# A new order, engine and bank table for a four-layer attention kernel on one core

## The chip, the core and the metric

The kernel runs on one core of a Trainium2 chip. The core has a matrix engine (TensorE, PE), a vector engine (VectorE, DVE), a scalar engine for activations (ScalarE, ACT), a general engine (GpSimd, POOL) and a sync engine (SyncE, SP), which issues most of the transfers. The engines run their own instruction streams in order and wait for each other through semaphores. Matmul results land in PSUM, which has eight banks of 128 partitions by 512 float32; everything else lives in SBUF. The metric is device time of the whole program in microseconds (us). The kernel before took 431.77 us (median of three, 431.07 to 432.0).

## The reference

x is 2048 tokens by 512 features, in bfloat16. Four residual layers follow each other, A, B, A, B, where both A layers share their weights and so do both B layers.

```python
x = x + _A_ref(_layernorm(x), A_wqkv, A_wo)
x = x + _B_ref(_layernorm(x), B_wqkv, B_wo)
x = x + _A_ref(_layernorm(x), A_wqkv, A_wo)
x = x + _B_ref(_layernorm(x), B_wqkv, B_wo)
```

Both have 32 heads of 16 features. Layer A is linear attention: phi(t) = where(t > 0, t + 1, exp(t)) + 1e-6 is applied to q and k; kv = sum over all tokens of phi(k) v; z = sum of phi(k); the output is phi(q) kv / (phi(q) z + 1e-6), times wo. Layer B is softmax attention with a causal window: a query sees its own key and the 255 before it, scores are scaled by 1/4.

## The kernel before

The 2048 tokens are 16 tiles of 128. The program is first written down as a graph of 2532 operations by the class Plan, in five parts:

- `layer_a_keys(1)`: for every tile, layernorm (`norm`: statistics on DVE, reciprocal root as `eps` and `pow` on POOL, `xn` on DVE, a transpose `T` by DMA on SP or by PE), keys and phi(k) (`a_k`, `phi`: `E` is the exp on ACT, `E1` and `phi` are on DVE), and the sums over tokens (`g`, `z`, then `gv`). Queries `a_q` go with it.
- `barrier(1)`: masks kv (`kvm`), multiplies it by wo (`M`), and forms the denominators (`den`, `rec`, `spread`, `pqd`).
- `middle(2)`: for each tile, the output of layer A (`aout`, `res`), the next norm, B's queries, keys and values (`bq`, `bk`, `bv` on PE; the copies out of PSUM `bqe`, `bke`, `bve` on ACT or DVE; `kd` and `vd` are SP transfers that spread keys and values), scores `s` and their exps `ex`, masks, values `pv` with division (`rcp`, `div`), the transpose `oT`, the projection `bout`, `res`, and then already the next A layer's norm and keys (and values `v`, copied by `ve`).
- `barrier(2)` and `middle(3)`: the same for the second pair of layers; each finished tile goes out by `outp` on POOL, and the last tile by `b_last` and `out` on SP.

Layer B's scores are computed transposed, with 64-key half blocks. `b_scores` (the near part: 256 queries from the block on) fills four PSUM banks per step by four row-tiled matmuls; two exps of 128x1024 read two banks each (line 609) and DVE multiplies the triangle by a mask (`mk`, line 615). `b_far` (lines 619 to 657) does the last 64 queries of the window; its exps are line 641 and its masks `mf` run on POOL (`affine_select`, line 649) or on DVE (a product, line 650). `b_values` (line 674) multiplies the exps by the values; the row of ones in the value tile gives the denominator.

The order is not computed when the kernel is built. `place` (line 88) decodes TABLE: for each position in the overall order the operation, for each operation its engine, for each PSUM tile its bank. It asserts that the order respects the graph and adds, for each tile, a dependency on the users of the tile that had the bank before. `synchronise` (line 123) turns dependencies between engines into semaphore waits, leaving out those that an earlier wait already covers; POOL's operations wait for each other one by one. `play` (line 912) emits each engine's share in this order. So what follows a waiting instruction on its engine waits as well. The keys in the code only describe the order; nothing reads them when a table is there.

Of the kernel before, what the change touches and what calls it, by code (L numbers as in the profile page):

```python
# [11 lines left out]
P = 128  # L12
# [3 lines left out]
T = 16  # L16
# [196 lines left out]
class Plan:  # L213
# [372 lines left out]
    def b_scores(self, j, b, fs, key):  # L586
# [6 lines left out]

        def put(e):
            m = None
            for i, f in enumerate(fs):
                for gq in range(4):
                    rows = slice(32 * gq, 32 * gq + 32)
                    m = e.matmul(K.ps(ps[gq])[:, ns * i:ns * i + ns], K.kB[rows, j % 4, 2 * f + b, :, :], K.XQ[rows, f, q:q + ns], start=True, stop=True, tile_position=(32 * gq, 0))  # L599
            return m  # L600
# [5 lines left out]
        for h in range(2):  # L606
            def ex(e, h=h):
                i = bass_view(K.PS[:, ps[2 * h].banks[0], :], [[512, 2], [ns, n], [1, ns]])
                return e.activation(out(2 * h, 2, ns), i, ACT.Exp, bias=0.0, scale=0.25)  # L609

            self.on("ACT", "ex", ex, key + 0.01 * h, act(2 * ns * n), wr=[("P", sl, f, b, h) for f in fs], rd=[("P", sl, f) for f in fs], ps=[ps[2 * h], ps[2 * h + 1]])
# [7 lines left out]
    def b_far(self, j, key):  # L619
# [3 lines left out]

        def put(e):
# [12 lines left out]
        far = lambda h: bass_view(K.P(sl)[:, 2 * h, 0, 256:320], [[704, 8], [384, 2], [1, 64]])  # L637
        for h in range(2):
            def ex(e, h=h):
                i = bass_view(K.PS[:, ps[2 * h].banks[0], :], [[128, 8], [64, 2], [1, 64]])  # L640
                return e.activation(far(h), i, ACT.Exp, bias=0.0, scale=0.25)  # L641
# [56 lines left out]
    def b_last(self, j, key):  # L698
# [4 lines left out]
        for h in range(2):  # L703
# [9 lines left out]
            self.copy("oTe", ps, lambda h=h: K.oT[:, s, h::2, :], lambda ps=ps: K.bf(ps, 256).rearrange("p (c n) -> p c n", c=2), key - 0.14 + 0.1 * h, 256, wr=[("oT", s, h)])  # L713
# [82 lines left out]
    r"c-rk(1Jq?nlFo<>WR`8)wr$(CZQHhO+qP|2wQYCpd+)ER>6z)7?d|Q|b9PU~|G&KV2EL5=B3_<%jfrF;8#GZ(6a&T@Hqi{3=q9BR6T`$bsZ44U",  # L796
    r"%cL=}O&pWf#5L)Rnmi_+NpJF+_@=$dVDg##CZkDUI+#JGqse3{nyIFk>0}C+X(qENXq-uCN}435kntv|8Emqc#wMKEX_}bCX1SSenwo4TndxkX",
    r"m>Fh;X=b{ZT_(IaZL*uLCWk3yikrgbuIXlSn&zgv*=_EbnI@6xVa}LbW|qlnhMJY;7gNr(Fsn>YGt8VdtIcq8-?TKn%tvO88DYws(xxPwGb7C?",
    r"6B&w_*=CO!ZO)rH=2w&4d~7b52d0l1W9FK@rnebuJ~1!NJ~PjJYSx;EX1-ZxN|<q`j7bXX%_FnGj5h{0n9s~YlMFVRYUXou(PW29X1^(GqQGU7",
    r"!W=N0%@vaz4w_OB6|S1crZhY;Dd3O+Xbgu<4TG@BJT*tmQIis)!58M4Nd>u0eRJJBHx*13^QCEJu9+9+D^tmof#_i2YZC)<Kuz<FA!uzFaza^n",  # L800
    r"$FwoIpd1J^fp1M)lN(ZlLLHL_(m*>?*QAB-jDrZKDWrqSCOyQ2dL|b1HMLD_=x5?Ud8lRjo48N`JWPa&kQWA+d=MWhK~Xc%#Do0M$Yg{JP#Gqe",
    r"MP{)n01Zq*SYir6LsJ+gnn`A<X$F&EnW+jbpbFH5de9MS!(_9?R5w#h9jI!ynodw3wwVUd5E{XD(;1GL=FkOpn3m8Ux<M;w3+<pQw1(rR4RnAT",
    r"=7i}1lVJ*UhovwTmcdDL2ByKg<}56SZE({}hf`(-yl1w<Ot@uMz${n^=U_Ihg73|0m;*bYC%kVKz#7;IYhfWAhudZm?1Emf8&1F;SPXOFB-}Cc",
    r"Afo9FKbXBRAI?J`*attFjnEG^!8-WBEP<cQX1D--;Ua{CQ*a4BH0vQ8{%peIWe5-b;R;m12rvK+!3H=C5g`I@fk$uzDq<vf0!Lv#RKf#r8XiML",
    r"{1C3fRyYVB!$)uzjzJ`>jFIskM8Rut1*771xDTH~G`xzR!&A5cpFkD73D@v5cnDST8C1htFbN;P3#g8h@eX_e@o@@1hZL9quVX5Vj_*JXjDZO;",
    r"B__d`*bozAGQ5F}a4O!0FJT}w#-un62f@4W6*R@^7z<}$226yhF*e@BjF=p6;d_t?;$SAs4DZ8COoLy;Ec^hnKwA6;vfyAyhjlP3WX1IO6V%0Q",
    r"P!qFZW^9J_uogDK7ML9uV{Kf5&G9yN!ljr4?_g)li7oMG$c0_-7s!pRups^lv#~YK!I$t9+u&UM7M`KOt{4vizlXbs_#ETnJ^T(VcEkHP4+(qV",
    r"4=^7KVO#8udGJRljP)@eR)Zqg0INe@EQ;;0J=TB)xB_cJ0w{((u{f^64p;ygYk}ZO?1%}W1S+n<)z}O3<610<z0qMQT!#;^5B9}Gum#uSVBCO-",
    r"VJmLKB(M=ZF2jeo376w$e1t<_JC??wPzIyfvKZYChY?T?ci=E60y{B=9fIX?DDJ|dFbs>qhZxh=wjbectYc%@;TYTQ!H+SH9f8GRFV?jq@mm~)",
    r"`*4AcYrn@55YH~O`|&%hXWzx-_9%XW@8Kdl8sEo$xY$0mi*Skk0Y}18`wrH(&ujxb3I<?*Y-q<|3LD>kfXi%3`y~#<WB4^bw}bFFCa_=O2|R#}",  # L810
    r"?5B7TM?+(~+<t?fVM2QdGuY4ZG5&}zY({$+U*Jjn2{YLz_ywl1@7SMlEWT?O;xCxij>98pZF74HGu!ca8gtn9Y&zS*PQcW5BA&sVHkD0p6WRA|",
    r"V%yT@vU%)T%wm(+y!ISswfSsEo6R<{*=;AA+cvfNE!k$av+ZixcC!Vn*e<raJ&$TH;IG)jUc`bnnSF_uu#LTpZLP6|th0S>Ve4%>8_t%r8*P6J",
    r"c9ZRA2U@i4ZFt+$4zerk0K3`tvV-k5o7DEUrR;V)#73~CZ6CYCma)6+P}{+lwY%*a`++TIciOeKyxn6f*dlhF9cGK#y>_J?ZY$bi_K+Q6E7?`{",
    r"h>d7V*wr?Y9cK^QG4Q1=ZpT7o`<2~lCqOFt+HSF_X*{&D<KURBY+KtX_JmDCRcusS)sD2s?T5CSU2m(~kL(6J+NP!Pc7jbuAKRlgJ)N@??I@dp",
    r"+EWM0NEhrR`-#m&pW2i5yxnIf+p%_vooe^nj`W%R$zHNw*aP;IJ!pTno#?dv#eQec*ex{8cBb#`S-X|G(69Eg%}rzMHu}NlAxn8F8%?)NUFk=g",
    r"ox0IWOLWoZpl__wb~4nR9POaYw3C25Wg(<p^tlx(Kw0UE{ni$ut2P|Xum$OwooS2Ebvw(3r=oPj&bBvg1e#-S*<w_IBGNY$i3(Fi>P^L|58bwv",
    r"s0`h)ed${&OC{(#ia{l*GL@t6X(;ue;gpZcQ&0MVO3{y$pLSCf8b&`+Y3fB)X(UynyS6%wrV(_{)}@~*CXJ$46q)YZ*ffB0QWSb%2hu}(l=e_m",
    r"8brq^4o#)wRF4MJ7@9_LDH_G2TvVSP+4wY_hENT9Y!gsTicSe>u5Cc`Y%MxK4XHmJr1`cEO{9L*hz`+Mnnb_Q6FZI?(+rwSP3RPjr@b_RPSX@h",
    r"MEmFrC8qs!j*?JQnn`Er0yU$gG>ekadAdcj3HT(<q1%Lfkrq*H61IGYu95Nyx<Sq9E;(*N*Xa^nrj~S*!gDKHOjjr(U!^6~nj&yyUP||98Aav$",
    r"w4Czs3W~xHXeGtwhm@Zq@pFp9tLRrMz%MB-&!yF5I62Luc$|WwaU1eHpHfnMK0<9N0WYMpe3;tNIZnur=mjkx=Ew97CE{?rhTf$ow3dk9qxX3o",  # L820
    r"CFc(~I<Kdc{60OS4RoGUa18!{I&n<?kUr$%9E(5V#9We}(#M>HOK@RM%}Kc+cjjbVgwyaf?!wo(D3{{${1I)W3j8q@<4shWEAnP4!-Y5%-{8tz",
    r"mM?H6uFB>3BH!dHe2IJWE$+kB_!GL#pHg4$&T08G>c>6#bNYnS@fXyCKjrjXoj>Cm+>0~taPG?e`Ewr0HTer3z#}*#*Wye(m<MtL&dguZARfx2",
    r"_$$i7mw5<(O<8#<U*Y9k!w%zRT${V`3a)9davdJcb$JXo<gr}KHsXa`pU3fH9?xI$B5ustxE^QcCY*ztGRQ`5#$WMf&dJSr32$PQuek-U<=p%Y",
    r"uj7`yh4b)w{+1_jUf#eHITugj?|3VJ&y#r@ujC*2N1no~cq(t_X}p75@oH|*cX&Fl;TilB-{pI}ldUwD`@D-E@NVA2E#x8Z<<|U&_i-DZ$1}MD",
    r"&*#UypWE^QCOOE5cow(g!#tax@DYB>3z+37pW<UYhv)KfKF!a#BR}U8e3D=A8GeV~<@fk!ZYFspkNm>L<X0{t;ib4lkfQRE3rPtv5>Z47O96=_",
    r"`6RNGl>DMnN(zdT($Z2|Nf~J^V`ZGglr~aUdP^T^E90e|#FF;XSC&W==^*{2qb!w9;w7r|mkBaJVoNs}D9fa~Oq9+tNG3@S2`7VPvUHK2GDPA?",
    r"Ihi6|rI!qqxDri<NqLzn!)1g_laW$EmP<t$CDCQNtdJ_QQpU(CsVp;OmduvXGE*wae5oo6WR9$sW3o{0$Xq!gG32f+lC5%F?#VpaCEMh_ES5bI",
    r"MYqcuiK@Hhft-?u5=}plM{-)CYZ)!8XC#K6lusq5K9&z9mX^~e@|k=t@g%m!m-3oecF0GvRuV`Yt)Tm4uT<1^@`db|N}5nM$a>i+N#uZ>m8bHt",
    r"B$8*6R1V5Uc`lb^lN^#{a#*fNa@i~|<Q+L8Tja7Fl`rL8`9$LCR}xRJ%KLIouE}|cuV2fLazPU4Mfq7OYf`-~-$*k3NfK&uttN@|S4pYW#b_1%",
    r"R=$(8@{7Ebbn?BtCpDz5{vhcEG?k{%dYVB}Yeu;tH>JL&QPEq1npjoSs@1AW>NK6QR@3mBUTdh=>RMAXXf~~-Q#FT9(~KHUhv;<8u8nl4HqlI)",  # L830
    r"Q-^70ZLGsJmqySmnny=yR*k45b(E%%+!{$!%4jX5sU)wC(d?31a!6!NBl)z57S`IDUz=)9X{H6Vffm(F(n1?*X2~T5^|mC@+|pdzX&oJ_?X`op",
    r")Z%(pi|IH$r&*+?bky-$N6za6tt%6?mSmMqI!SBG9__5zWUqG761q=kX-VC$v-NW=rC;bA?W(=Bw0^1eq>oP416p6Y=@dPvy>*@*(yz3YF3`E!",
    r"TEEuA`i*wiBicZ|)%n^++v+m?PSdy*+Cyh(PfhC<Y7_UpF4umV&Rx=`F1@>=i?qM?)n;z7Ue*k5l`heln$aEAmAYCpxutqco4XUbMq9XRdR$w&",
    r"liJGN(5pH?*Xlq$rPp<n4$>d=jBe4J`lGgXr*)lXcAIsu{-pPGz24Vt`m=7(3;IBR(T#dhAL*|O?ul+!bhq@eS|=`xd#Jb7xu?2S^SV2#?yiP&",
    r"`CNGSO!K=o?zu*AwcHD3m({(awOvG)&3&Za?a(?dyL(r6D!KQxo{Qvmsd4XXEca5|x;U<#`%ojh_Aa*T=c2gXn!`nP{asGi)zx*m+yEENb#u|(",
    r"#~Rmtpxxak8p9=WpK1q}$0czcT}+qTeWvkTCzse2a`D|jSJ)+R1zl2C#1(S|TtZjEC3g*_s7vM=NpaU$=C~$O&dqgArMz3~=DBsQf-C8Ix%sY?",
    r">+Ke}^{%vA==!)tu97R`Qn=1;v8&=zy0UJG>+7z#RIaj{<gU7ku8T|Urno`wnj7pUyQ*%RyY8yF?QV!0>Z-dNZil<+M!BA@hP&mQuj$4(?{B-Q",
    r"ZmGND!uio|m|Nz;`w?!MTj6@R<!+@L?l!qqu87~_#=4?@wTs|Kx`_U%tM7KYNPe^1=Zg7f?tmNTwz}tTyxZ?0`*&S&AI0x-@3{%CgrDekyOREW",
    r"SISR!huj`_*X?zOU1@*M9dv7419#sYai`n{_knBZHoDU;sz2%)xoG~3`_?sf(fu*^y*uvCxd-k$cf!5nzH}$uL-)d+bzi#~?!0^CX1cH3hi;aO",
    r";XiVZ-48CN|Hj4jv)#uomjBho^Do^e?nhU~$M-)u<J0+{T^#?Z`^9DO=s$DmeIgG&f&bi9^<TKeKB2$hF1n2ViA&;>`Ag3FYCeT8>#O^6KDJNp",  # L840
    r"lln})yszLh`-(oL@8c`^EWVcS>udW|KCAEN>-b!rd}W{8v#;x`_|#r}9^cHT@#?erw7!MU?(_QQzMik?bNHOTfv@3P`O7Z9Z|xWRmVSxP=iB)D",
    r"exPsb+xbDhp>OY(`oVsz@8BExj((hP?8p0|zKI{;hxh`1xG(4@_@=&)ALhIJiGGqF;n(>7zOY~GNBYTrlwaqk_)dPbpXxjNF@C+D=DYY6e!5@g",
    r"d-xfCrSIx{`gy*WU*%`|ZhpC+<#+hizPI1tcln)uqo3`!_)UJZ-|FZ1qkgyF=I8slet|#kxBFv$p+D*O_|yJ`Kjkm_Gk&kX<QMtN{;J>S&-(rT",
# [170 lines left out]
```

## Time and profile before

| what | us |
|---|---|
| whole program, median of 3 | 431.77 |
| profiled execution, span | 428.2 |
| PE busy | 392.7 |
| DVE busy | 356.2 |
| ACT busy | 347.4 |
| POOL busy | 128.6 |
| first exp of the first B layer | 69.0 |
| last exp of the first B layer ends | 234.8 |
| first exp of the second B layer | 269.7 |
| last exp of the second B layer ends | 419.3 |

The page gives the profiled execution by its span, 428.2 us from the first instruction to the last; the unprofiled runs' median lies 3.6 us above it. Times of instructions count from the start of the span. Busy time of PE is that of matmuls, whose ends are modelled, so a PE that is shown busy is not always at its peak. The slices on the page are 10.7 us each. The granted clock is the share of its full clock that PE was given.

### The profile page before, as it was taken

The page shows a single profiled execution, that of the slowest core. Times are in us where ns is not written, and L with a number is a line of the kernel's source. Part 1 is how long each engine was busy: PE and PEld are TensorE (multiplying, and loading weights), DVE is VectorE, ACT ScalarE, POOL GpSimd, SP SyncE. Part 2 cuts the span into 40 slices and gives each one's busy share as a digit, 9 for nine tenths or more (in the row PEclk, how much of TensorE's full clock was granted, in tenths as well). Part 3 has the DMA queues.
Part 4 walks back from the last instruction along what each step waited for, and adds up shares of the span by engine and source line. Part 5 has one row for each costly group of instructions (what it writes and reads, how often), then busy time and mean ns, then how long its engine had stood idle before and what let it go on. Part 6 is the DMA issues. An engine that isn't in the chain of part 4 may idle for free.

```text
span 428.2 us, 17035 instructions
## 1 busy us (share of the span) xinstructions
PE 392.7 (92%) x7471; PEld 257.9 (60%) x7548; DVE 356.2 (83%) x796; ACT 347.4 (81%) x433; POOL 128.6 (30%) x223
## 2 busy tenths in 40 slices
PE   8899999999899999999999999999889979997775
PEld 3445676766465566565565768585657746765544
DVE  6998899998998799887887789998798699875564
ACT  2423547999899999999998164999999999999992
POOL 4789322101240233130503303212144324332000
PEclk9999999999999999999999999999999999999968
DMA  7933016432153533453324000452434522553222
GB/s 248 269 74 87 2 42 160 117 90 70 39 111 64 103 103 77 91 112 55 95 47 65 19 2 26 114 120 63 113 62 106 116 77 77 116 133 102 64 52 51
DMA packets 66978, 37.81 MB, mean 88 GB/s; under 512 B 48248, under 2 KB 61816, under 8 KB 66904
## 3 DMA queue, kind: packets, MB, share of 16 engines
q1 hardware_dynamic: 66176, 34.75, 34.7%
q0 software_dynamic: 720, 1.97, 1.3%
q8 instruction: 59, 0.97, 1.0%
q14 instruction: 15, 0.12, 0.1%
q10 hardware_dynamic: 8, 0.00, 0.0%
HBM read 6.29 MB, written 2.10 MB: 20 GB/s over the span
## 4 chain that ended last, share of the span: by engine, by line
PE 42%; ACT 35%; DVE 16%; issue 4%; DMA 3%; POOL 1%; POOLq 0%; ACTq 0%
ACT pb L609 23%; PE ps L369 14%; PE ps L383 11%; PE ps L674 7%; ACT pb L641 6%; PE ps L599 4%; ACT vp L609 3%; DVE stats L330 2%; DVE XQ L526 2%; DVE vp L394 2%; ACT tE L392 1%; DVE tE L393 1%; DVE vp L334 1%; DMA xT<-xn 1%; DVE xres L537 1%
## 5 line engine op out<-in xcount | busy, mean ns | idle before, releaser
L609 ACT ACTIVATE pb<-ps 128x1024 bf16<-128x1024 f32 (+2 forms) x224 | 207.0, 1039 | 7.5 <-PE ps L599 6.1
L674 PEld LDWEIGHTS ps<-vB,pb 128*128 128x128 bf16 x2560 | 78.0, 96 | 13.0 <-DVE pb L615 2.8
L674 PE MATMUL ps<-vB,pb 128*128 128x34 bf16 x2560 | 83.6, 178 | 2.0 <-DVE pb L615 1.1
L392 ACT ACTIVATE tE<-ps 128x512 bf16<-128x512 f32 x64 | 38.8, 609 | 41.0 <-PE ps L369 20.6
L383 PE MATMUL ps<-xT,wBp 128*128 128x128 bf16 x1024 | 69.5, 219 | 2.1 <-DMA xT<-xn 0.8
L332 POOL TENSOR_SCALAR ve<-mv 128x1 f32<-128x1 f32 x64 | 16.6, 260 | 174.0 <-DVE mv L331 172.4
L383 PEld LDWEIGHTS ps<-xT,wBp 128*128 128x128 bf16 x1024 | 58.9, 98 | 14.8 <-issue 3.6
L615 DVE TENSOR_TENSOR pb<-pb,tri 128x512 bf16<-128x512 bf16 x112 | 48.0, 436 | 12.3 <-ACT pb L609 11.6
L599 PE MATMUL ps<-XQ,kB 32*128 32x256 bf16 (+2 forms) x1024 | 50.1, 270 | 6.9 <-ACT pb L609 3.4
L641 ACT ACTIVATE pb<-ps 128x1024 bf16<-128x1024 f32 x50 | 49.4, 1061 | 1.1 <-PE ps L632 1.0
L369 PE MATMUL ps<-wA,XQ 128*128 128x512 bf16 x177 | 46.3, 380 | 3.6 <-DVE vp L394 0.7
L537 DVE TENSOR_TENSOR xres<-ps,xres 128x512 bf16<-128x512 f32 x63 | 43.0, 685 | 7.3 <-PE ps L369 6.4
L649 POOL TENSOR_SCALAR_AFFINE_SELECT pb<-pb 128x1024 bf16<-128x1024 bf16 x30 | 35.3, 1175 | 38.5 <-ACT pb L641 37.3
L330 DVE BATCH_NORM_STATS2 stats<-xres 128x6 f32<-128x512 bf16 x64 | 43.1, 680 | 2.6 <-DMA xres<-in_A_x_dram 2.0
L333 POOL TENSOR_TENSOR rs<-ve,negh 128x1 f32<-128x1 f32 x64 | 37.5, 586 | 5.3
L383 PE MATMUL ps<-XQ,wA 128*128 128x128 bf16 x512 | 36.1, 219 | 0.4 <-DVE vp L394 0.2
L599 PEld LDWEIGHTS ps<-XQ,kB 32*128 32x128 bf16 x1024 | 15.5, 92 | 33.8 <-ACT pb L609 14.9
L369 PE MATMUL ps<-M,XQ 128*128 128x512 bf16 x115 | 31.7, 381 | 4.0 <-DVE XQ L526 1.6
L383 PEld LDWEIGHTS ps<-XQ,wA 128*128 128x128 bf16 x512 | 30.6, 98 | 7.7 <-DVE vp L394 1.2
L369 PE MATMUL ps<-wBo,oT 128*128 128x512 bf16 x104 | 30.1, 395 | 3.4 <-ACT pb L609 0.9
L369 PE MATMUL ps<-wBv,xT 128*128 128x512 bf16 x106 | 30.7, 381 | 2.7 <-issue 0.8
L369 PEld LDWEIGHTS ps<-wA,XQ 128*128 128x128 bf16 x192 | 16.1, 98 | 21.5 <-ACT XQ L353 1.7
(109 smaller groups left out, 541.2 us busy)
## 6 DMA issues: line engine op xcount, KB each, us to landing
vB<-vS SPq DMA_DIRECT2D x64, 136.0 KB, 2.5
kB<-vp SPq DMA_DIRECT2D x64, 128.0 KB, 2.2
out_dram<-xres POOLq DMA_DIRECT2D x15, 128.0 KB, 2.3
wA<-in_A_wqkv_dram SPq DMA_DIRECT2D x3, 512.0 KB, 5.9
xres<-in_A_x_dram SPq DMA_DIRECT2D x2, 512.0 KB, 4.9
pb<-in_B_wqkv_dram SPq DMA_DIRECT2D x1, 1024.0 KB, 9.0
xres<-in_A_x_dram SPq DMA_DIRECT2D x3, 256.0 KB, 4.9
wAo<-in_A_wo_dram SPq DMA_DIRECT2D x1, 512.0 KB, 7.4
```

What stands on the lines that cost most here:

```text
L330: self.on("DVE", "stats", lambda e: e.bn_stats(K.stats[:, t, :], K.xres[:, t, :]), key, dve(512), rd=[("xres", t)], wr=[("stats", t)])
L333: self.pow = self.on("POOL", "pow", lambda e: e.tensor_tensor(K.rs[:, t, :], K.ve[:, t, :], K.negh[:], ALU.pow), key + 0.03, (640, 690), r ...
L369: m = e.matmul(K.ps(ps), lhs(c), rhs(c), start=c == 0, stop=c == 3)
L383: m = e.matmul(K.ps(ps)[:, f * P:(f + 1) * P], w(c, f), xT(c), start=c == 0, stop=c == 3)
L392: self.on("ACT", "E", lambda e: e.activation(K.tE[:, s, :], K.ps(ps), ACT.Exp, bias=0.0), key, act(512), wr=[("tE", s)], ps=[ps])
L537: self.on("DVE", "res", lambda e: e.tensor_tensor(K.xres[:, t, :], K.ps(po), K.xres[:, t, :], ALU.add), key, dve(512), rd=[("xres", t)], w ...
L599: m = e.matmul(K.ps(ps[gq])[:, ns * i:ns * i + ns], K.kB[rows, j % 4, 2 * f + b, :, :], K.XQ[rows, f, q:q + ns], start=True, stop=True, ti ...
L609: return e.activation(out(2 * h, 2, ns), i, ACT.Exp, bias=0.0, scale=0.25)
L615: return e.tensor_tensor(x, x, K.tri[:, 0, :].unsqueeze(1).unsqueeze(1).to_broadcast([P, 4, n, 64]), ALU.mult)
L641: return e.activation(far(h), i, ACT.Exp, bias=0.0, scale=0.25)
L649: return e.affine_select(out=x, in_=x, compare_op=ALU.is_ge, fill=0.0, base=-2, pattern=[[0, 16], [-2, 64]], channel_multiplier=1)
L674: m = e.matmul(K.ps(ps)[:, 34 * u:34 * u + 34], K.P((b // 2) % rp)[:, gq, f, o:o + P], K.vB[:, (b // 2) % 4, b % 2, r, :], start=i == 0, s ...
```

## The change

The table of order, engines and banks is another one. The number of operations and what each computes stay as they were. Read out of the two tables:

| engine | operations before | after | mean move of an operation in its engine's order |
|---|---|---|---|
| PE | 858 | 858 | 3.3 places |
| ACT | 432 | 428 | 2.2 |
| DVE | 795 | 788 | 5.9 |
| POOL | 219 | 230 | 7.4 |
| SP | 228 | 228 | 1.9 |

49 operations change engine: of the far masks `mf`, 15 go from DVE to POOL and 4 from POOL to DVE; of the copies out of PSUM, `bke` 5 go from ACT to DVE and 2 back, `ve` 4 and 1, `bve` 2 and 2, `bqe` 2 and 3, `ge` 2 and 1, `recb` 2 to DVE, and `Te` 3 and `Me` 1 to ACT. Banks: before, exps read the pairs 0-1, 2-3, 4-5 or 6-7; after, any two neighbouring banks.

Beside the table three lines change. The exps' input access pattern takes the distance of its two banks from the table (`pair`) in place of a fixed 512; the far exps' output pattern is written with one dimension more, over the same elements; and in `b_last` the two copies `oTe` are ordered behind earlier users of the same slot of oT.

```diff
@@ b_scores
+        pair = lambda two, free: bass_view(K.PS[:, two[0].banks[0], :], [[512 * (two[1].banks[0] - two[0].banks[0]), 2]] + free)
...
-                i = bass_view(K.PS[:, ps[2 * h].banks[0], :], [[512, 2], [ns, n], [1, ns]])
+                i = pair(ps[2 * h:2 * h + 2], [[ns, n], [1, ns]])
@@ b_far
-        far = lambda h: bass_view(K.P(sl)[:, 2 * h, 0, 256:320], [[704, 8], [384, 2], [1, 64]])
+        far = lambda h: bass_view(K.P(sl)[:, 2 * h, 0, 256:320], [[2816, 2], [704, 4], [384, 2], [1, 64]])
...
-                i = bass_view(K.PS[:, ps[2 * h].banks[0], :], [[128, 8], [64, 2], [1, 64]])
+                i = pair(ps[2 * h:2 * h + 2], [[128, 4], [64, 2], [1, 64]])
@@ b_last
-            self.copy("oTe", ps, lambda h=h: K.oT[:, s, h::2, :], lambda ps=ps: K.bf(ps, 256).rearrange("p (c n) -> p c n", c=2), key - 0.14 + 0.1 * h, 256, wr=[("oT", s, h)])
+            self.copy("oTe", ps, lambda h=h: K.oT[:, s, h::2, :], lambda ps=ps: K.bf(ps, 256).rearrange("p (c n) -> p c n", c=2), key - 0.14 + 0.1 * h, 256, wr=[("oT", s, h)] + ([] if h else [("oT", s)]), rd=[("oT", s)] if h else [])
@@ TABLE
-    r"c-rk(1Jq?nlFo<>WR`8)wr$(CZQHhO+qP|2wQYCpd+)ER>6z)7?d|Q|b9PU~|G&KV2EL5=B3_<%jfrF;8#GZ(6a&T@Hqi{3=q9BR6T`$bsZ44U",
...
+    r"c-q}~1N<#Xk9LwuDpl9EZQHhO+qP}nwr$(C@7VUt{Z60%%(wII&O7^RcYnKmPoJ(%rJg)_l2iZg3lIaML3D@(u^|q`1p}RdAT6YWE?{9bq=yU;54r-v8",
...
```

## The prediction

> **What bounds the kernel now.** I read the page's forty slices first, then cut the span at the first and last exp of each windowed-attention layer and asked for the busy time of those stretches. Columns there: length, then busy microseconds and instructions of PE, weight loads, DVE, ACT and POOL, then granted clock, DMA share, GB/s.
>
> ```profile
> span 428.2 us, 17035 instructions
> PE 392.7 (92%) x7471; PEld 257.9 (60%) x7548; DVE 356.2 (83%) x796; ACT 347.4 (81%) x433; POOL 128.6 (30%) x223
> ...
> PE   8899999999899999999999999999889979997775
> ...
> PEclk9999999999999999999999999999999999999968
> ```
>
> ```profile
> 69.00:234.80 165.80, 155.90 (x3158) 101.02 (x3190) 144.92 (x332) 157.59 (x189) 41.46 (x68) 1.00 0.38 84
> 234.80:269.70 34.90, 33.74 (x568) 25.82 (x572) 29.67 (x67) 15.28 (x29) 8.13 (x15) 1.00 0.08 24
> 269.70:419.30 149.60, 134.63 (x3044) 91.48 (x3070) 116.95 (x255) 145.77 (x168) 40.29 (x57) 0.97 0.39 93
> 419.30:428.20 8.90, 4.21 (x88) 2.82 (x85) 3.36 (x9) 0.77 (x2) 0.54 (x1) 0.88 0.20 46
> 0.00:42.80 42.80, 38.69 (x260) 18.45 (x266) 36.58 (x87) 14.99 (x25) 31.71 (x70) 1.00 0.62 170
> 42.80:69.00 26.20, 25.54 (x366) 18.31 (x369) 24.73 (x51) 13.00 (x24) 6.42 (x13) 1.00 0.22 52
> ```
>
> The reader should see four regimes. In the two attention stretches (165.8 and 149.6 us) ACT is idle for only 8.2 and 3.8 us, so these last as long as ACT's work. Between them lie 34.9 us of which PE is busy 33.7 and ACT 15.3. Ahead of the first exp there are 42.8 us set by DVE (36.6 busy; 3.0 of the rest are the first load) and 26.2 set by PE. The last 8.9 us are a chain. The page's chain agrees:
>
> ```profile
> PE 42%; ACT 35%; DVE 16%; issue 4%; DMA 3%; POOL 1%; POOLq 0%; ACTq 0%
> ```
>
> The whole program has a median of 431.8 us, 3.6 more than the profiled span; I sum against the span and add the 3.6.
>
> **The change part by part.** I read both tables as lists: which operation stands where on which engine. The scores keep their order but for one exchange; a PE operation moves 3.3 places on average, ACT 2.2, DVE 5.9, POOL 7.4, SP 1.9. So this is the old schedule, permuted locally. PE durations below are issue rates from the chain's rows (16 matmuls of 128 columns in 0.89 to 1.00 us, four of 512 in 0.86 to 0.97), others are each instruction's own record.
>
> *Start to the first exp.* Ahead of the first scores PE loses three halves of attention-A outputs and two of B keys (2.3 us) and gains two of B values (0.9): -1.4. DVE's work ahead of the first mask falls by 0.9 (73.9 to 73.0). Against it: on SP the key weights wAk go from third to fifth load, behind 512 KB more (tiles 2 and 3, and 6 and 7, 256 KB each); at the 248 and 269 GB/s of the page's first two slices that is 2.0 us. DVE can use the time for statistics of tiles that arrive earlier. On POOL, the last copy of the B query weights now stands behind the rsqrt of the first two B norms (57.0 to 59.5 us before), and the first query matmul waits for them; it fed a copy at 62.7, so there is about a microsecond of room. I take -1.0; bounds -4.6 (the 3.2 us of DVE's other idle time and the 1.4) to +2.0 (the load is exposed whole).
>
> *First attention layer.* ACT loses three value copies, two key copies, one of B values, one of queries and an E (5.5 us by their records), and gains two queries, two keys, an E and a value copy (4.0). ACT sets this stretch: -1.5. Its bounds are those of ACT's idle time there, taken up under the rivals.
>
> *Between the layers.* PE loses two halves each of bk, bq, q and gains four of q: -1.0, in the stretch where PE is busy 33.7 of 34.9. The key and query halves reappear in the next stretch, where PE has 15 us idle. If ACT or DVE were late instead, the gain is 0.
>
> *Second attention layer.* ACT loses two key copies, one B value copy and a reciprocal copy and gains a key and a query copy: 3.0 against 1.7, -1.3.
>
> *Masks of the far keys.* Of 56, POOL did 35, now 46: 15 go from DVE, 4 to it. DVE saves 11 x 0.68 = 7.5 us; POOL takes 11 x 1.15 = 12.6, of which it has plenty. But the two disturb each other:
>
> ```profile
> L649 POOL TENSOR_SCALAR_AFFINE_SELECT pb<-pb x30: 1136/1147/1659, 98.7 to 381.9; 128x1024 bf16<-128x1024 bf16 x30
> ...
> L615 DVE TENSOR_TENSOR pb<-pb,tri x112: 359/416/1376, 73.2 to 415.2; 128x512 bf16<-128x512 bf16 x112
> ```
>
> The near mask (minimum/median/maximum ns) takes 416 and once 1376. Laid beside POOL's far masks in time, seven near masks average 0.84 us, three normalisations 1.21 against 0.40, two min-adds 0.73 against 0.28; copies from PSUM are unmoved. That is 6.3 us of DVE for 35, 0.18 each, so 11 more cost 2.0. DVE has 20.9 and 32.7 us idle in the two stretches: the net 5.5 of relief is worth 0 here, hidden by ACT; if DVE were the bound it would be the whole 5.5, and if every new mask hit a neighbour by the largest excess seen (0.96) it would cost 10.6 of the idle 53.6. [...]
>
> *Waits.* PE's semaphore waits beyond the first of an operation, each an instruction of its own, go from 162 to 244. The 144 that the trace shows last 51 ns each: 82 are 4.2 us of PE's queue. 73 are in the attention stretches, behind ACT: 0. Nine are in the PE-bound ones: +0.5. Bounds 0 to +4.2.
>
> *The end.* PE is given more to do late: after the scores at 12.25 of the last layer 26.4 us of work remain where 23.0 did (bq, bk, bv, a pv). The order of the last 15 PE operations is the same, so the 8.9 us stay. The clock may not:
>
> ```profile
> 395.90:406.20 10.30, 7.68 (x239) 5.52 (x241) 5.34 (x15) 10.30 (x13) 0.54 (x1) 1.00 0.31 68
> 406.20:409.60 3.40, 3.07 (x58) 1.56 (x59) 1.71 (x6) 3.36 (x4) 0.00 (x0) 0.50 0.31 69
> 409.60:413.00 3.40, 2.38 (x96) 1.75 (x88) 1.90 (x5) 3.09 (x5) 0.54 (x1) 0.99 0.37 100
> 413.00:419.80 6.80, 5.47 (x128) 3.80 (x130) 5.13 (x12) 5.51 (x11) 0.54 (x1) 0.50 0.07 22
> ```
>
> The granted clock halves twice after PE has been only three quarters busy. On the chain that stretches 48 small matmuls to 1.48 us (1.19 elsewhere) and two projections to 1.48 and 1.50 (0.81): 1.65 us. With PE fuller I take -0.5, between 0 and -1.65. [...]
>
> SP also moves the second half of the last tile's key spread from 390 us to behind two transposes of o (issue near 410, landing 2.2 median, 4.0 at most, needed near 414.5); it is what would be late next. Outputs on POOL are deferred to about 418, hidden by the tail. The far exps' pattern has one dimension more for the same 1024 elements; far exps average 1061 ns and near ones 1066 with fewer dimensions, so 0. All pairs of banks are neighbours in both tables: 0.
>
> Sum: -1.0 - 1.5 - 1.0 - 1.3 + 0.5 - 0.5 = -4.8: span 423.4, time 427.0.
>
> **The rivals.**
> *Idle time also goes* (faster). ACT's 12.0 us of idle in the attention stretches halve: another -6.0, 421.0. For it: eight gaps of 0.55 to 0.89 us between ACT instructions, mostly in front of an exp, which order alone can close. Against: nothing in the lists shows that the closed ones are not replaced.
>
> *PE held by a POOL mask* (slower). PE takes its queue in order; 13 of its operations wait for POOL now, 25 after, 22 of them value matmuls. Where POOL's mask stands behind an output DMA or a norm whose data is late, the value matmuls hold the next scores and ACT runs dry. A gap of that kind is 0.69 us (mean of those eight). Twelve cost 8.3: 435.3. It decides from seven on (4.8 / 0.69). For it: POOL waited 172 us in all at the norms' eps. Against: far masks are due two blocks later.
>
> *No change to be seen*: the moved copies lay beside ACT's waits and the new waits eat the rest: 431.8, within 0.9 (0.2%, about what a measurement of this kernel can tell from no change).
>
> **How the numbers follow.** The forecast 0.37 (own range 424 to 430.5), idle gone too 0.20, no change 0.08, slower 0.35: an order that already keeps ACT 95 to 97% busy has more ways to lose than to gain, so the slower case weighs nearly as much as the forecast. Faster 0.57, same 0.08, slower 0.35. The range runs from 419.5 (the idle-gone case with 1.5 us more of what the start's lower bound allows) to 436.0 (the slower rival with 0.7 us more of the waits' 4.2).
>
> **What would show it.** Right: first exp near 68, the layers' stretches 164 and 148 long, the middle 34, a clock above 0.66 in the last slices. Wrong: more ACT idle before exps whose scores stand behind value matmuls waiting for POOL; near masks over 0.8 us more often than now; the first query copy later than 62.7; scores of the last tile waiting for the key spread.

## The result and the profile after

The changed kernel takes 424.74 us (median of four, 423.75 to 426.87) against 431.42 us for the kernel before in the same comparison: a ratio of 0.985, 95% interval 0.9815 to 0.9884. Run again unaltered beside the last experiments it took 426.56 us, a ratio of 0.9868 (0.9835 to 0.9902). So it is faster by 5 to 7 us, where 4.8 had been forecast.

The page of the changed kernel's first profile, to be read beside the page lines of the prediction:

```profile
span 424.9 us, 17140 instructions
PE 390.1 (92%) x7479; PEld 260.1 (61%) x7548; DVE 355.9 (84%) x789; ACT 345.4 (81%) x429; POOL 141.5 (33%) x234
...
PE   5999999999899989999998999999999978999875
...
PEclk8799999999999999999999999999999999999999
...
PE 55%; ACT 24%; DVE 11%; issue 4%; DMA 4%; POOL 1%; SPq 0%; POOLq 0%; DVEq 0%
```

The busy sums hardly moved: DVE -0.3, ACT -2.0, POOL +12.9. What changed is the chain: PE's share is 55% instead of 42, ACT's 24 instead of 35. The share of the whole span differs from profile to profile (the old order with extra matmuls near its end, further down, has 55% and 23% too). Cut at 268 us, about where the second B layer begins, PE's share is 50% before, and 53% and 52% in two later kernels that are the old one up to there, against 71% and 74% in the two profiles of the changed kernel. And the clock digits are other ones: low at the start in place of the end.

One thing has to be known before PE's times are read. The profile of before has records of 7471 matmuls to 7548 weight loads, and this one of 7479; all later profiles have one for one (7548 to 7548 in the second profile of the changed kernel). Nearly all that are missing in the profile of before have 512 columns, some 0.2 us each (four in 0.86 to 0.97 us). So in these two profiles PE's busy time is too low and its idle time too high.

The next two answers cut this profile, and that of the second run of the same kernel, at the same events as the prediction did: first B layer, middle, second B layer, end. Columns are again length, busy time of PE, weight loads, DVE, ACT, POOL, then clock, DMA share, GB/s.

```profile
68.30:232.50 164.20, 154.99 (x3172) 102.90 (x3205) 146.12 (x329) 156.38 (x187) 49.58 (x75) 1.00 0.39 85
232.50:265.80 33.30, 32.44 (x539) 24.31 (x543) 29.18 (x64) 15.57 (x29) 6.90 (x14) 1.00 0.11 28
265.80:416.10 150.30, 135.59 (x3084) 92.88 (x3106) 121.54 (x259) 145.42 (x167) 47.05 (x64) 1.00 0.37 92
416.10:424.90 8.80, 4.14 (x86) 2.76 (x83) 3.35 (x9) 0.77 (x3) 0.54 (x1) 0.99 0.27 64
```

```profile
67.70:231.30 163.60, 159.54 (x3207) 103.27 (x3206) 144.81 (x329) 156.45 (x187) 49.47 (x75) 1.00 0.40 86
231.30:264.40 33.10, 32.63 (x544) 24.23 (x542) 29.23 (x64) 15.55 (x29) 6.84 (x14) 1.00 0.10 26
264.40:415.00 150.60, 139.50 (x3105) 93.38 (x3104) 121.54 (x258) 145.27 (x166) 46.98 (x64) 0.99 0.37 92
415.00:424.10 9.10, 4.63 (x87) 3.06 (x84) 3.35 (x9) 0.78 (x3) 0.54 (x1) 0.82 0.24 62
```

| stretch | before | after | after, second profile |
|---|---|---|---|
| start to first exp | 69.0 | 68.3 | 67.7 |
| first B layer | 165.8 | 164.2 | 163.6 |
| middle | 34.9 | 33.3 | 33.1 |
| second B layer | 149.6 | 150.3 | 150.6 |
| end | 8.9 | 8.8 | 9.1 |
| span | 428.2 | 424.9 | 424.1 |

Start, first layer and middle got shorter, by 3.9 and 5.3 us in all. The second layer is longer by about 1 us than in the profile of before. The spans differ by 3.3 and 4.1 us, less than the medians do. The profile of before was a short draw: in the runs of that kernel listed with the experiments the time lies 1.7 to 1.8 us above the span, so a median run of some 431.5 us has a span near 429.8, not 428.2. (The 3.6 us that the prediction put around the span were two things: some 1.8 around it, and a profiled execution 1.6 to 1.8 us shorter than the usual one.) Two kernels below that begin with the old table repeat its start, first layer and middle (69.3, 165.5, 34.6 and 68.6, 165.5, 34.7), so by exclusion the missing 1.6 us sit in the second layer and the end of an ordinary run of before. No profile shows them, and so the growth of the second layer by 1 us is not established either.

### The profile page after: what moved, and what is told of

Same layout as the page of the kernel before. It is cut to its first block, busy times and chain, and to the rows that moved or that the text cites. A ratio compares the mean times of both kernels' runs of the same rounds, so it can differ in the third digit from the quotient of the medians.

```text
span 424.9 us, 17140 instructions
## 1 busy us (share of the span) xinstructions
PE 390.1 (92%) x7479; PEld 260.1 (61%) x7548; DVE 355.9 (84%) x789; ACT 345.4 (81%) x429; POOL 141.5 (33%) x234
## 4 chain that ended last, share of the span: by engine, by line
PE 55%; ACT 24%; DVE 11%; issue 4%; DMA 4%; POOL 1%; SPq 0%; POOLq 0%; DVEq 0%
PE ps L369 20%; ACT pb L611 16%; PE ps L383 15%; PE ps L678 8%; PE ps L601 5%; ACT pb L645 3%; PE ps L444 3%; ACT vp L611 2%; DVE XQ L526 2%; DMA wA<-in_A_wqkv_dram 2%; DVE pb L617 1%; DVE xres L537 1%; PE ps L636 1%; DVE xn L334 1%; DMA oT<-o 1%
## 5 line engine op out<-in xcount | busy, mean ns | idle before, releaser
L332 POOL TENSOR_SCALAR ve<-mv 128x1 f32<-128x1 f32 x64 | 15.7, 246 | 187.8 <-DVE mv L331 174.7
L653 POOL TENSOR_SCALAR_AFFINE_SELECT pb<-pb 128x1024 bf16<-128x1024 bf16 x41 | 48.3, 1178 | 61.5 <-ACT pb L645 60.0
L392 ACT ACTIVATE tE<-ps 128x512 bf16<-128x512 f32 x64 | 37.8, 603 | 35.3 <-PE ps L369 16.2
L617 DVE TENSOR_TENSOR pb<-pb,tri 128x512 bf16<-128x512 bf16 x112 | 51.5, 470 | 6.6 <-ACT pb L611 6.2
L333 POOL TENSOR_TENSOR rs<-ve,negh 128x1 f32<-128x1 f32 x64 | 38.4, 599 | 5.2
L383 PE MATMUL ps<-XQ,wA 128*128 128x128 bf16 x512 | 34.3, 219 | 0.0
L369 PE MATMUL ps<-M,XQ 128*128 128x512 bf16 x113 | 30.2, 380 | 2.6 <-issue 0.8
L369 PEld LDWEIGHTS ps<-wA,XQ 128*128 128x128 bf16 x192 | 17.0, 99 | 20.5 <-issue 2.2
```

Of the source, the lines that this page charges most:

```text
L333: self.pow = self.on("POOL", "pow", lambda e: e.tensor_tensor(K.rs[:, t, :], K.ve[:, t, :], K.negh[:], ALU.pow), key + 0.03, (640, 690), r ...
L369: m = e.matmul(K.ps(ps), lhs(c), rhs(c), start=c == 0, stop=c == 3)
L383: m = e.matmul(K.ps(ps)[:, f * P:(f + 1) * P], w(c, f), xT(c), start=c == 0, stop=c == 3)
L392: self.on("ACT", "E", lambda e: e.activation(K.tE[:, s, :], K.ps(ps), ACT.Exp, bias=0.0), key, act(512), wr=[("tE", s)], ps=[ps])
L617: return e.tensor_tensor(x, x, K.tri[:, 0, :].unsqueeze(1).unsqueeze(1).to_broadcast([P, 4, n, 64]), ALU.mult)
L653: return e.affine_select(out=x, in_=x, compare_op=ALU.is_ge, fill=0.0, base=-2, pattern=[[0, 16], [-2, 64]], channel_multiplier=1)
```

## The experiments

The table has three parts, order, engines and banks, so old and new parts can be joined to one table wherever the joined order still respects the graph and the banks. In the diffs "old" and "new" mean the tables before and after. All these kernels compute the whole reference.

**Engines without the order.**

```diff
- order old, engines old, banks old
+ order old, engines new, banks old
```

> The old order and the old banks with the new engine of each of the 49 operations. Forecast's theory (ACT's own work sets the attention layers): 2.8 us of copies leave ACT there, so 428.6 us against 431.4, ACT idle in the two layers as before (8.2 and 3.8 us). Rival (the engine moves pay only inside the new order): 431 to 434, with ACT idle time up by what its work fell. [...]

Measured: 438.81 us, ratio 1.016 (1.0124 to 1.0197). The copies did leave ACT (187 instructions instead of 189 in the first layer, 165 instead of 168 in the second), but in the first layer its busy time stayed at 157.7 us, and that layer lasts 171.2 us instead of 165.8, with 13.5 us of ACT idle in place of 8.2. The rival has the sign right and half the size: in the old order the new places cost 7 us. Which waits carry them was not traced. Of the near masks, nine take over 0.55 us, where five did in the kernel before.

**The order without the engines.**

```diff
- order old, engines old, banks old
+ order new, engines old, banks new
```

> The new order and the new banks with the old engine of each operation. Forecast's theory: loses the 2.8 us of ACT copies and keeps the rest, 427.5 us. Rival (the order carries all of it): 424.7, within 0.9 of the changed kernel. A third way (order and engines need each other): over 431.

Measured: 456.09 us, ratio 1.0553 (1.052 to 1.0587). All three expectations are far off in size, and the third has the sign right: 30 us above the changed kernel. ACT idles 20.6 us in the first B layer. Order and engines are one thing here: each half alone loses, both together gain. The new banks come with the new order in every kernel here, so what they are worth by themselves is not known.

**Which of the engines.** Two kernels keep the new order and put back one group each.

```diff
- engines new
+ engines new, but the 19 moved far masks (mf) where they were
```

> The changed kernel with the 19 far masks that changed engine put back (POOL 35, DVE 21). Forecast: the masks' places are worth 0 because ACT hides DVE's 5.5 us: 424.7 within 0.9. Rival after the two halves (the old engines in the new order cost 31 us): the order counts on them, DVE's masks stand ahead of others in its queue and POOL's old ones behind data that come late: 430 to 440, with ACT idle in the B layers up by that.

Measured: 443.56 us, ratio 1.0275 (1.0246 to 1.0304), 18 us above the changed kernel. The cut of its profile shows where (first B layer, then the second):

```profile
67.10:242.50 175.40, 163.72 (x3207) 104.85 (x3206) 149.32 (x336) 157.04 (x187) 41.25 (x68) 0.97 0.35 80
...
275.60:431.10 155.50, 140.40 (x3103) 94.49 (x3102) 120.52 (x262) 145.52 (x166) 42.36 (x60) 0.98 0.37 89
```

ACT's busy time is nearly that of the changed kernel (157.04 and 145.52 against 156.38 and 145.42), and yet the layers are 11 and 5 us longer. DVE has 26 us idle in the first of them, so it is not short of time either. The waits of PE name the step:

```profile
PE ps L678 <- DVE pb L654: 9.0, 4, 2.9
...
PE ps L678 <- DVE vp L654: 2.3, 1, 2.3
```

Line 678 is the value matmuls, line 654 the far mask on DVE. In the new order such a mask stands where POOL reaches it in time; on DVE the same place lies behind other work. Five of the moved masks stand right ahead of the value matmuls that read them, and five times such a matmul waits, 1.4 to 2.9 us each, 11.3 us in all. One of the five:

```profile
304.17 0.69 DVE L537 TENSOR_TENSOR xres<-ps,xres 128x512 bf16<-128x512 f32 x1 [0.28 <-PE ps L369]
304.89 0.69 DVE L330 BATCH_NORM_STATS2 stats<-xres 128x6 f32<-128x512 bf16 x1
...
305.72 0.66 DVE L654 TENSOR_TENSOR pb<-pb,tri 128x1024 bf16<-128x1024 bf16 x1
...
306.43 0.77 PE L678 MATMUL ps<-vB,pb 128*128 128x34 bf16 x24 [2.31 <-DVE pb L654]
...
307.13 0.40 PE L601 MATMUL ps<-XQ,kB 32*128 32x256 bf16 x8
...
307.58 1.02 ACT L611 ACTIVATE pb<-ps 128x1024 bf16<-128x1024 f32 x1 [1.90 <-PE ps L601]
```

The mask stands behind a residual sum and the statistics of a norm. PE is in order, so the next scores (line 601) wait too, and ACT runs dry behind them. The kernel with the order alone has the same five waits. In the first layer three of them make 6.6 of the 11 us; half-clock windows of 6.8 and 3.4 us begin at two of the waits there, and how much of the rest is theirs was not separated. In the changed kernel the same masks on POOL make PE wait once (second profile):

```profile
L653 POOL TENSOR_SCALAR_AFFINE_SELECT pb<-pb x41: 1144/1146/1431, 93.0 to 409.7; 128x1024 bf16<-128x1024 bf16 x41
...
who waited for it (us, times):
  PEld ps L678: 0.3, 1
```

```diff
- engines new
+ engines new, but the 21 moved copies bqe, bke, bve, ve where they were
```

> The changed kernel with the 22 copies out of PSUM in the B layers (queries, keys, B values, A values) that changed engine put back. Forecast's theory: ACT gets about 2.4 us of work back and the layers last that much longer: 427.2. Rival (like the masks, the copies' places are part of the order: moved back alone they stand behind work of the other engine that comes later): 430 to 440, more than the sum of the copies. If the copies do not matter: 424.7 within 0.9.

Measured: 434.0 us, ratio 1.0051 (1.0026 to 1.0075), 7 to 8 us above the changed kernel where 2.4 us of work were expected (the tables give 21 copies, not the 22 of the expectation). The first layer lasts 167.2 us instead of 163.6 with ACT 157.8 busy instead of 156.4: of 3.6 us, 1.4 are work and the rest is new waiting, middle and second layer lose 1.1 and 2.2 more, start 1.3. Of the second layer's 2.2 us, 1.8 are ACT's work (147.1 instead of 145.3). So the total is the rival's, more than the sum of the copies, but in the two layers over half of the loss is ACT's own work.

**One stretch at a time.** Three kernels change table at a seam.

```diff
+ old up to the first scores of the first B layer, new from there
```

> The old order, engines and banks up to the first scores, the new ones from there on (the banks of the old part renamed so that they meet). Forecast's theory: the new start is worth 1.0, so 425.7. Rival one (the start is worth 3 us where its clock is not cold): 427.7. Rival two (the new start, whose first key matmul comes at 9.5 us instead of 6.6 because its weights are the fifth load, is no gain at all): 423 to 424.7, a version that beats both.

Measured: 428.53 us, ratio 0.9927 (0.9903 to 0.9951), 2 to 4 us above the changed kernel and nearest to rival one. But its profile does not put the loss in the start: the first exp comes at 68.4 us, as in the changed kernel's first profile, and the first layer lasts 165.9 us instead of 163.6 to 164.2.

```diff
+ old up to the first scores of the second B layer, new from there
```

> The old order, engines and banks up to the first scores of the second B layer, the new ones from there to the end. Forecast's theory: second layer -1.3, waits and clock together about 0: 430.1 us. Rival read from the two profiles (the new second layer lasts 150.3 us against 149.6): 431.4 to 432.1. Clock: if the new order alone keeps the clock up, the half clock after 406 us is gone from this run.

Measured: 432.01 us, ratio 1.0008 (0.9985 to 1.0031). The new second layer is worth nothing by itself: it lasts 151.7 us here. The clock's sign came: the half clock after 406 us is gone but for 3.4 us near 420, and the granted clock of the twelve runs is 0.994 to 0.999, where runs of the kernel before have 0.978 to 0.992. The time is the old one all the same.

```diff
+ new up to the first scores of the second B layer, old from there
```

> The changed kernel up to the first scores of the second B layer, the old order, engines and banks from there on (banks keep their numbers). With the mirror run at 432.0 (0.5 above the kernel before) the new second layer is worth nothing or less: 424.2, within 0.9 of the changed kernel, perhaps a little better than both. Forecast's theory (second layer -1.3): 426.0. If the clock of the last 25 us counts: the half clock after 395 us comes back and the run is 1 to 3 us above the changed kernel.

Measured: 429.65 us, ratio 0.9947 (0.9926 to 0.9968), so 3 to 5 us above the changed kernel. This one and its mirror should add up to the whole change and do not: -2.3 and +0.3 against -5.7 to -6.5. Its first layer and middle are those of the changed kernel (163.3 and 33.1), its second layer lasts 153.3, longer than in either. So a seam costs something of its own: work that the first table had put off falls on the second, which does not expect it (3110 weight loads there instead of 3070). The clock is as low as the old one's, 0.978 to 0.992, with half-clock windows of 3.4 us at 349.5, 397.3 and 414.4 us, as the expectation on the clock had it. The stretches' worth can be read from these three as bounds only: the new parts up to the second layer are worth at least 2.3 us, the start at most some 3.

**The start.** In the changed kernel's first profile the first key matmul came at 9.5 us, 2.9 us later than before. Of these, 2.1 us are the first transpose, which came at 7.5 us instead of 5.4 and waited for DVE; then the matmul waited 1.2 us for its weights, now the fifth load. In the second profile it came at 8.4 us and did not wait for them.

```diff
- loads: x0, x2, x1, x6, wAk, ...
+ loads: x0, x2, wAk, x1, x6, ...
```

> The changed kernel with the key weights wAk as third load (behind x0 and tiles 2 and 3) in place of fifth, nothing else. Theory one (the late weights are paid: the first key matmul came at 9.5 us instead of 6.6 and PE fell to half clock from 8.4 to 15.2 in the profiled run): first key matmul near 7.5, no cold window at the start, 1 to 2.5 us faster than the changed kernel, 422 to 424. Theory two (the start is set by DVE's statistics and the order of the tiles' loads, the weights lie beside): within 0.9 of 424.7. Theory three: tile 1 and tiles 6 and 7 come later for it and DVE waits for them: 425.5 to 427.

Measured: 426.8 us, ratio 0.9889 (0.9861 to 0.9917), beside 0.9848 for the next kernel in the same batch. Not faster, and by the profiles slower: the first exp comes at 69.8 us, against 68.3 in the first profile of the changed kernel, which had a half clock of the same length at the same place. PE's timeline of this kernel shows theory three at work:

```profile
8.88 0.61 PE L346 MATMUL ps<-ident,vp 128*128 128x128 bf16 x4 [4.03 <-DVE vp L334]
...
10.17 1.04 PE L369 MATMUL ps<-wA,XQ 128*128 128x512 bf16 x2
```

and that of the changed kernel:

```profile
7.46 0.40 PE L346 MATMUL ps<-ident,vp 128*128 128x128 bf16 x4 [2.27 <-DVE vp L334]
...
9.52 1.01 PE L369 MATMUL ps<-wA,XQ 128*128 128x512 bf16 x2 [1.23 <-DMA wA<-in_A_wqkv_dram]
```

The weights are no longer waited for, but the first transpose comes 1.4 us later. It waits for DVE, where tile 0's normalisation stands behind the statistics of tiles 3, 1 and 6, and tile 1 is now loaded after 512 KB of weights: DVE waits 2.06 us for it. The start hangs on the tiles' loads, and the late weights cost little.

```diff
-                    for _ in range(9):
+                    for _ in range(18):
...
-FILL, SPARE = {1: 2, 4: 1, 6: 6}, 6
+FILL, SPARE = {1: 8, 4: 1, 6: 6}, 6
```

> The changed kernel with 18 in place of 9 dummy matmuls ahead of PE's first operation and 8 in place of 2 behind its first transpose, so that PE does not pause at 5.2 to 7.5 and 8.3 to 9.5 us; they compute nothing that is used. If the half clock at the start is what the profiled run of the changed kernel lost against its other runs (its span 424.9 against 421.9 to 422.8): clock 1.0 up to the end in every run, median 423.5 to 424.7, the spread smaller. If the clock at the start is hidden under DVE: no change. If the dummies delay the first keys: 425 to 426.

Measured: 424.77 us, ratio 0.9848 (0.982 to 0.9876): no change, although the half clock at the start is gone and the first exp comes at 67.5. The half clock there costs some 0.8 us at most, the difference between 68.3 and 67.5. The clock was not full to the end, as the expectation asked: windows of 3.4 us stand at 349 and 414 us.

**The control.**

```diff
  the changed kernel, no edit
```

> The changed kernel unaltered, as the control of this batch and for a second profile of it. If its first profile was a slow draw at the start only (half clock from 8.4 to 15.2 us): 424 to 425 us, first exp near 66 to 67 where the start's clock is full, the first B layer near 163, the middle near 33, the second layer near 150. If the gain on the chip comes from elsewhere than start, first layer and middle, those stretches repeat the first profile's and another one is shorter.

Measured: 426.56 us, ratio 0.9868 (0.9835 to 0.9902). The stretches repeat the first profile's within 0.7 us (table above). The time is above the 424 to 425 us expected, and the start's clock was not full either: a half-clock window of 3.4 us stands at 8.7 us.

**The clock and PE's room.** In `b_values` of the last layer:

```diff
-                for gq in range(4):
+                for gq in [0, 1, 2, 3] * (2 if rp == 4 and j >= 11 else 1):
```

> The kernel before, with the value matmuls of the last five tiles of the second B layer done twice into the same columns (the second pass starts each sum anew, so nothing else changes): ten operations of 24 matmuls at 25 ns, 6 us more of PE's work between about 375 and 420 us. If the half clock after 406 us costs the kernel before 1.5 us or more: the half clock is gone or shorter and the time rises by at least 1.5 us less than with the same edit in the changed kernel, perhaps falls below 431.5. If the half clock lies beside ACT's work: both kernels lose the same.

> The same doubled value matmuls in the changed kernel, whose clock is full there already: it shows the price of the extra work alone. ACT sets this stretch, PE has room: 424.7 to 427; if PE's queue holds the scores back, up to 6 us more than the changed kernel.

Measured: 440.04 us (ratio 1.0184, 1.0146 to 1.0221) from the kernel before, 437.51 us (1.0122, 1.0085 to 1.0159) from the changed one. The extra work is twice what the expectation says: 20 operations of 24 matmuls, 480 in all (8028 in the traces instead of 7548), an estimated 12 us at 25 ns (48 took 1.19 us on the chain of the kernel before). They cost the old order about 8 us and the new one about 11. Both numbers matter. First, they show that PE has next to no room in the last third of the second layer. Here is the second layer of the new order with the doubled matmuls:

```profile
266.10:425.50 159.40, 148.57 (x3487) 102.65 (x3486) 120.76 (x259) 146.29 (x166) 46.84 (x64) 0.99 0.35 88
```

Beside the row 264.40:415.00 of the changed kernel PE is busy 9.1 us more, the stretch is 8.8 us longer, and PE's idle time is 10.8 us where it was 11.1. ACT has 1 us more of work and is idle 13.1 us instead of 5.3. The other 2.3 us fall into the end (11.4 us instead of 9.1). The old order with the doubled matmuls, and the part that had the half clock:

```profile
268.80:427.00 158.20, 146.89 (x3459) 100.89 (x3458) 116.46 (x255) 146.74 (x168) 40.25 (x57) 0.99 0.37 89
...
395.00:420.00 25.00, 20.26 (x655) 15.52 (x651) 10.40 (x25) 20.01 (x23) 1.08 (x2) 1.00 0.34 69
```

ACT again has 1 us more of work, and the stretch grew from 149.6 to 158.2. Second, the half clock of 406 us and after is gone, as the expectation's first case had it (a window of 3.4 us stands at 349.7 instead), and the old order lost some 3 us less than the new one (the two intervals leave 0.4 to 6). That is on the clock's side, but it is no proof: the new order has PE fuller there from the start, so the same matmuls may simply cost it more.

## Why the prediction was right, and which steps were not

*Direction and size.* 427.0 us was forecast and 424.7 measured, 426.6 in the repeat. The forecast ratio of 0.989 lies inside the repeat's interval and just above the first one's. The first three terms, -3.5 together, came out as -3.9 and -5.3. The others, -1.3 together, are not settled: the whole gain of 5.7 to 6.5 us leaves them 0.4 to 2.6 us. That the sum came out close is in part luck, since one reading that it rests on was wrong.

*The reading of what bounds.* "These last as long as ACT's work" was too simple. PE's idle time in the two attention stretches, 9.9 and 15.0 us by the rows of the prediction, is too high: there the profile has 32 and 26 matmuls fewer than weight loads. The kernel before with the doubled matmuls is the old one up to the second B layer and lacks none:

```profile
68.60:234.10 165.50, 160.12 (x3192) 101.14 (x3191) 145.00 (x332) 157.53 (x190) 41.39 (x68) 1.00 0.38 84
234.10:268.80 34.70, 34.20 (x573) 25.73 (x571) 29.47 (x67) 15.08 (x28) 8.12 (x15) 1.00 0.09 25
```

In the first B layer PE is idle for 5.4 us there and ACT for 8.0. PE is the fuller of the two.

*Start, -1.0.* Measured -0.7 and -1.3. The late weights, the term's risk, are nearly free, as the wAk kernel and the second profile show. The first query copy, named as a sign, comes at 62.2 and 61.6 instead of 62.7, so POOL's late copy of the query weights holds nothing up.

*First layer, -1.5.* Measured -1.6 and -2.2. ACT's busy time fell by 1.2, its idle time from 8.2 to 7.8 and 7.2. Beside the first row above, PE's busy time fell by 0.6, to 159.5, and its idle time from 5.4 to 4.1 in the second profile. So the size is right; that ACT's work alone sets it is not shown. The step's size was a little high in one place: the moved copies were counted by their records, 0.68 us on average in the kernel before, while behind 17 of ACT's 35 copies there the next instruction starts before the record ends, 0.56 us after the copy's own start on average.

*Middle, -1.0.* Measured -1.6 and -1.8. Beside the second row above, PE's busy time fell by 1.6 us in the second profile, to 32.6, and the stretch by as much, from 34.7 to 33.1. Right, and somewhat more.

*Second layer, -1.3: its cover was wrong, its size is open.* It grew by 0.7 to 1.0 against the profile of before, which was a short draw there; the medians leave 0.4 to 2.6 us of gain to this layer, the end and the clock together. Behind the old parts the new second layer is worth nothing; behind the new parts the old one costs 3 to 5 us, both with a seam. What failed is the cover given to the PE work moved out of the middle, "in the next stretch, where PE has 15 us idle", and with it the reading that ACT alone sets that stretch. The 15 us are some 11 (11.1 in the second profile of the changed kernel, which lacks no matmul), and they are not room: 9.1 us of doubled matmuls made the stretch 8.8 us longer and left PE's idle time as it was. PE is in order and the scores, which ACT needs, stand behind whatever was added. ACT's work counts there as well (1.8 us more of it in the copies kernel, 2.2 us of time), but it fell by only 0.4 us in the changed kernel. The two halves each of bk and bq that came into this stretch are 1.9 us of PE's work; what they cost, no run separates.

*Masks, 0.* The term as a net sum is not contradicted: ACT's idle time in the layers is 12.7 and 12.5 us after, 12.0 before. DVE's price beside POOL's masks was right in kind. The near mask's rows in the second profile:

```profile
L617 DVE TENSOR_TENSOR pb<-pb,tri x112: 364/417/1817, 73.0 to 411.8; 128x512 bf16<-128x512 bf16 x112
```

The median is unmoved, the longest is 1817 ns instead of 1376, and all near masks together take 59.5 to 60.3 us instead of 55.9; three or two more of them than before exceed 0.8 us. The 2.0 us expected for eleven more masks were 3.6 to 4.3 in near masks alone, all inside DVE's idle time. Within these 1817 ns, 1.40 us over the median, POOL ran a far mask of 1.16 us, and the near mask ended 0.28 us after it. But nine of the 20 near masks that overlap a far mask in that profile take no more than 0.55 us. In the first profile of the changed kernel the 108 near masks that overlap none take 427 ns at most, in that of before the 121 such take 426. How the two engines disturb each other, no run shows. What the term missed is that a mask's engine is not free to choose: with the old engines for the masks alone the new order loses 18 us. "Worth 0" held for the pair of order and place, not for the place.

*Waits, +0.5.* No run separates it; 82 more wait instructions did not show.

*Clock, -0.5.* The new kernel's profiles have full clock from 395 to 413 us where the old one had half from 406 to 410 and from 413 to 420; in the repeat a half window of 3.4 us remains near 415. The granted clock of whole runs is 0.979 to 0.991 (the middle eight tenths of 57 runs of before, median 0.986), against a median of 0.994 in the ten runs of the changed kernel. Over the 57 runs the time falls by 1.3 us per 0.01 of clock (correlation -0.45), which would make the 0.008 worth 1.1 us. Whether the clock falls because PE waits, or PE is late because the clock falls, these runs do not decide. Against a worth of its own speaks the kernel with the new table from the second B layer on: 0.994 to 0.999 of clock, and no time gained, though it pays for a seam too. The size of this term stays open between 0 and the 3 us of the doubled matmuls.

*The rivals.* "PE held by a POOL mask" did not happen: one wait of 0.3 us in place of twelve of 0.69. Its mechanism is real, though, and appeared when masks were moved without the order; there DVE was the engine that came late. "Idle time also goes" did not happen either; ACT's idle time in the layers is the same. "No change" is excluded by both intervals.

No kernel tried here beats the changed one beyond the intervals; the one with more dummy matmuls at the start equals it.

## What to carry to other kernels

Where an order is written out for in-order queues, an operation's engine and its place in the order are one decision: price them together, since moving one back alone cost 7 to 30 us here while both together gained 6. Idle time on an engine is room only if what stands behind the added work can wait; in a queue that feeds another full engine it may be none: here 11 us idle took up 0.3 of 9.1 us of added work. And before a sum is made against a profile, check how the profiled execution stands among the runs (here it was 1.6 us short of the usual one) and whether its matmuls are as many as its weight loads.

## What the runs showed of the hardware

The granted clock differs between executions of one and the same program: 0.978 to 0.992 for the kernel before, 0.988 to 1.000 for the changed one, with half-clock windows of 3.4 us or twice that. Some stand behind a pause: at the start of the changed kernel, where PE had just waited 2.27 us, and, with the masks moved back, at its waits of 2.9 and 2.4 us. Others do not: in the 3.4 us ahead of the drops at 406.2 and 413.0 us of the kernel before PE was busy for 2.51 and 2.38 us, ahead of the one at 350.0 us in the second profile of the changed kernel for 1.76, and no gap in these was longer than 0.81 us. So these figures give no one length of pause behind which the clock falls. At the start a window of 6.8 us cost at most 0.8 us (first exp at 68.3 us with it, at 67.5 without).

In the kernel with the key weights as third load, their place in the queue mattered more for the transfers behind them than for their own reader: 512 KB of weights ahead of tile 1 (128 KB) and of tiles 6 and 7 (256 KB) ended PE's wait of 1.23 us for the weights and delayed the first transpose by 1.4 us (8.88 instead of 7.46), which waited for tile 1's statistics.
